# Two unused tiles that move every loaded tile to a multiple of 512 bytes of its partition, in a one-token decoder block

## The chip, the cores and the metric

The kernel runs on one core of a Trainium2 chip. The metric is the device time of one execution in microseconds (us), lower is better. Three runs before the change gave 672.55, 671.69 and 673.35 us, a median of 672.55 us.

## What is computed

One decoding step of a conditioned transformer block for 4 sequences of one token each, with a model width of 512. The condition `c` gives six vectors (shifts, scales and gates). The attention has 32 heads of 128 with a cache of 4096 keys and values for each head and sequence; the caches are 128 MiB each, and every byte of both is read once.

```python
mod = (silu(c) @ w_mod).reshape(4, 6, 1, 512)        # sa, ca, ga, sb, cb, gb
h = layernorm(x) * (1 + ca) + sa
q = (h @ wq) split into 32 heads of 128
p = softmax(q . k_cache / sqrt(128)); o = p . v_cache
x = x + ga * (o @ wo)
h = layernorm(x) * (1 + cb) + sb
z = gelu(h @ w_in); z1, z2 = halves; z2 = layernorm(z2)
x = x + gb * ((z1 * (w_sp * z2 + b_sp)) @ w_out)
```

All arrays are bfloat16.

## The kernel before, in words

The attention is cut into 32 steps (`NT`), one for each pair of four heads and one sequence. A step needs one key tile `kt` and one value tile `vt`, each 128 partitions x 128 rows x 128 numbers of bfloat16: 4096 KB, and 32,768 bytes in one piece for each partition, in HBM as in SBUF. Both names have two buffers (pool `kv`). The order of all work is written out by hand (`manual_schedule`); nothing is rearranged by a scheduler.

In step `i` VectorE multiplies the key tile in place by the queries, in two halves (`mult`, L286, 64 instructions in all). TensorE adds up groups of 8 of the products with an identity matrix as weights, 16 matmuls for each half (`reduce_d`, L292, 1024 in all). VectorE finishes the sum (L301) and takes maxima, ScalarE takes exponentials into `pbd` (L324), and two steps later TensorE multiplies with the value tile (`pv`, L352). As soon as the second half of `reduce_d` of step `i` is issued, the load of key tile `i + 2` is issued into the buffer that step `i` has read (`load_k`, L103), and after `pv(i - 2)` the load of value tile `i` (`load_v`, L103). All these loads go through the queue of SyncE (SP) in the order in which they stand, and an issue that waits for its buffer holds back those behind it.

Ahead of the caches `w_mod` (`wm_sb`, L89) and `wq` (`wq_sb`, L91) are loaded. In step 2 their pool is closed, and `wo_sb` and `wo_last` (L530, L535) are loaded into its place; ahead of the last step the last value tile (in four pieces, `TAIL`), `win_sb` (L552) and `wout_sb` (L554) follow. After the last landing the gated second half of the block is finished (L630 to L695).

SBUF is laid out by pools: first `consts` (constants, `pbd`, queries `qbc` and small vectors), then `kv`, then `work`, and then `pre`, whose place `wts` takes over. Within a pool tiles lie one behind the other, in sizes rounded up to 32 bytes. So the start of every loaded tile follows from the sum of the sizes ahead of it:

| tiles | pool | start in the partition, before | modulo 512 |
|---|---|---|---|
| `kt` (two buffers) | kv | 35,360 and 68,128 | 32 |
| `vt` (two buffers) | kv | 100,896 and 133,664 | 32 |
| `wm_sb`, later `wo_sb` | pre, wts | 169,440 | 480 |
| `wq_sb` | pre | 194,016 | 480 |
| `wo_last`, `win_sb`, `wout_sb` | wts | 198,112, 202,208, 216,544 | 480 |

Of the kernel before, what the change touches and what calls it, by code (L numbers as in the profile page):

```python
# [24 lines left out]
def kernel(  # L25
# [17 lines left out]
    P = 128  # L43
# [21 lines left out]
    consts = ctx.enter_context(tc.tile_pool(name="consts", bufs=1))  # L65
    kvp = ctx.enter_context(tc.tile_pool(name="kv", bufs=2))
    wk = ctx.enter_context(tc.tile_pool(name="work", bufs=2))
# [97 lines left out]
    x1w = consts.tile([P, DJ, R], F32, name="x1w")  # L165
    nc.gpsimd.memset(x1w, 0.0)
    cT = consts.tile([P, DJ, B], BF16, name="cT")
    pbds, opss = [], []
    for k in range(3):
        t = consts.tile([P, NJ, HQ], BF16, name=f"pbd{k}")  # L170
# [555 lines left out]
```

## Time and profile before

| | us |
|---|---|
| median of three runs | 672.55 |
| the profiled execution's own time | 671.79 |
| its span, first to last instruction | 670.0 |
| VectorE busy | 415.3 (62%) |
| TensorE (matmul) busy | 388.6 (58%) |
| ScalarE busy | 85.0 (13%) |
| DMA queue of SyncE, share of 16 DMA engines' span | 98.6% |

The span is what the trace covers; 1.79 us of the profiled execution's time lie around it. Busy times are sums over one engine. The share of the DMA queue is the time that its packets took, divided by 16 times the span, since a core has 16 DMA engines. "GB/s" is what the DMA engines moved in a stretch. In the groups of instructions a row has the line, engine and operation, output and inputs with shapes, the count, the busy time, the mean of one in ns, and the idle time of the engine ahead of them with what ended it.

### The profile page before, as it was taken

The page shows a single profiled execution, that of the slowest core. Times are in us where ns is not written, and L with a number is a line of the kernel's source. Part 1 is how long each engine was busy: PE and PEld are TensorE (multiplying, and loading weights), DVE is VectorE, ACT ScalarE, POOL GpSimd, SP SyncE. Part 2 cuts the span into 40 slices and gives each one's busy share as a digit, 9 for nine tenths or more (in the row PEclk, how much of TensorE's full clock was granted, in tenths as well). Part 3 has the DMA queues.
Part 4 walks back from the last instruction along what each step waited for, and adds up shares of the span by engine and source line. Part 5 has one row for each costly group of instructions (what it writes and reads, how often), then busy time and mean ns, then how long its engine had stood idle before and what let it go on. Part 6 is the DMA issues. An engine that isn't in the chain of part 4 may idle for free.

```text
span 670.0 us, 6859 instructions
## 1 busy us (share of the span) xinstructions
PE 388.6 (58%) x2864; PEld 182.6 (27%) x2864; DVE 415.3 (62%) x594; ACT 85.0 (13%) x278; POOL 3.8 (1%) x17
## 2 busy tenths in 40 slices
PE   1184784455566655646664566566555566556666
PEld 1032332122222322222222233222222233222335
DVE  3185593775555776555577656557765555776833
ACT  1011220111011111101111110111111011111112
POOL 1000000000000000000000000000000000000000
PEclk9998988778988778789877789987777988877975
DMA  9999999999999999999999999999999999999995
GB/s 376 432 432 425 430 418 426 435 434 427 426 435 431 431 428 427 433 430 431 428 433 430 432 426 431 435 426 430 434 430 432 426 431 430 429 432 423 439 413 203
DMA packets 12322, 283.17 MB, mean 423 GB/s; under 512 B 1276, under 2 KB 2692, under 8 KB 3076
## 3 DMA queue, kind: packets, MB, share of 16 engines
q1 hardware_dynamic: 12272, 282.73, 98.6%
q8 instruction: 22, 0.36, 0.2%
q14 instruction: 8, 0.07, 0.0%
q10 hardware_dynamic: 20, 0.01, 0.0%
HBM read 282.73 MB, written 0.00 MB: 422 GB/s over the span
## 4 chain that ended last, share of the span: by engine, by line
DMA 58%; DVE 28%; PE 12%; issue 1%; SPq 0%; DVEq 0%
DMA kt<-in_A_k_cache_dram 53%; DVE kt L286 21%; PE red L292 10%; DMA wout_sb<-in_B_w_out_dram 5%; DVE osb L364 2%; DVE S L301 1%; DVE mrow L310 1%; DVE osb L360 1%; PE ops L352 1%; DVE mt L314 0%; DVE nM L316 0%; PE qps L272 0%; DVE mb L312 0%; DVE nM L317 0%; PE sm L240 0%
## 5 line engine op out<-in xcount | busy, mean ns | idle before, releaser
L292 PE MATMUL red<-kt,ident_bf 128*128 128x512 bf16 x1024 | 292.1, 450 | 251.3 <-DVE kt L286 251.3
L286 DVE TENSOR_TENSOR kt<-kt,qbc 128x8192 bf16<-128x8192 bf16 x64 | 282.8, 4420 | 201.9 <-DMA kt<-in_A_k_cache_dram 201.0
L292 PEld LDWEIGHTS <-ident_bf 128*128 128x128 bf16 x1024 | 116.7, 114 | 419.2 <-issue 275.2
L324 ACT ACTIVATE pbd<-S,nM 32x128 bf16<-32x128 f32 x128 | 73.8, 577 | 508.3 <-DVE rz L344 470.7
L352 PE MATMUL ops<-vt,pbd 128*16 128x512 bf16 x992 | 60.9, 387 | 0.0
L301 DVE TENSOR_REDUCE S<-red 128x64 f32<-128x512 f32 x64 | 43.6, 682 | 5.2 <-PE red L292 5.2
L364 DVE SCALAR_TENSOR_TENSOR osb<-ops,selg,osb 128x128 f32<-128x128 f32 x93 | 32.6, 351 | 3.3
L324 ACT ACTIVATION_READ_ACCUMULATOR pbd<-S,nM 32x1 f32 x128 | 32.0, 250 | 0.0
L352 PEld LDWEIGHTS <-pbd 128*16 128x16 bf16 x992 | 24.1, 90 | 21.6 <-issue 1.7
L372 PEld LDWEIGHTS sm<-sel,osb 128*128 128x128 f32 x62 | 11.9, 198 | 11.1 <-DVE osb L364 4.5
L272 PE MATMUL qps<-wq_sb,hTb 128*32 128x512 bf16 x128 | 9.2, 412 | 9.2 <-DMA wq_sb<-in_A_wq_dram 8.5
L339 PEld LDWEIGHTS sm<-rsb,ones_f 128*128 128x128 f32 x64 | 12.3, 194 | 4.5
L372 PE MATMUL sm<-sel,osb 128*128 128x4 f32 x62 | 9.3, 221 | 5.4 <-DVE osb L364 5.4
L360 DVE TENSOR_SCALAR osb<-ops,selg 128x128 f32<-128x128 f32 x31 | 10.2, 328 | 3.4 <-PE ops L352 3.4
L276 ACT CAST qbc<-qps 128x512 bf16<-128x512 f32 x8 | 4.7, 586 | 46.6 <-PE qps L272 46.6
L310 DVE TENSOR_REDUCE mrow<-S 128x1 f32<-128x128 f32 x32 | 9.1, 286 | 1.1
L339 PE MATMUL sm<-rsb,ones_f 128*128 128x4 f32 x64 | 9.3, 215 | 0.0
L332 DVE TENSOR_SCALAR rsb<-mask,rs 128x4 f32<-128x4 f32 x32 | 7.1, 223 | 2.4 <-ACT pbd L324 2.4
L314 DVE STREAM_TRANSPOSE mt<-mb 128x32 f32<-128x32 f32 x32 | 6.8, 212 | 1.1
L272 PEld LDWEIGHTS <-hTb 128*32 128x32 bf16 x128 | 3.1, 100 | 13.3 <-issue 10.6
L316 DVE TENSOR_REDUCE nM<-mt 128x1 f32<-128x32 f32 x32 | 6.0, 186 | 1.1
L312 DVE COPY mb<-mrow 128x32 f32<-128x32 f32 x32 | 5.8, 181 | 1.1
(129 smaller groups left out, 86.5 us busy)
## 6 DMA issues: line engine op xcount, KB each, us to landing
kt<-in_A_k_cache_dram SPq DMA_DIRECT2D x31, 4096.0 KB, 23.3
vt<-in_A_v_cache_dram SPq DMA_DIRECT2D x31, 4096.0 KB, 30.9
wq_sb<-in_A_wq_dram SPq DMA_DIRECT2D x1, 4096.0 KB
kt<-in_A_k_cache_dram SPq DMA_DIRECT2D x2, 2048.0 KB, 18.3
wm_sb<-in_w_mod_dram SPq DMA_DIRECT2D x1, 3072.0 KB, 10.4
wo_sb<-in_A_wo_dram SPq DMA_DIRECT2D x3, 1024.0 KB, 23.1
kt<-in_A_v_cache_dram SPq DMA_DIRECT2D x1, 2048.0 KB
win_sb<-in_B_w_in_dram SPq DMA_DIRECT2D x1, 1792.0 KB, 33.5
```

What stands on the lines that cost most here:

```text
L272: nc.tensor.matmul(qp[R * q:R * (q + 1)], lhsT=hTb[:, k, b, :], rhs=wq_v[:, k, gs, q, :], start=(k == 0), stop=(k == DJ - 1), tile_positio ...
L286: nc.vector.tensor_tensor(out=kt, in0=kt, in1=bc(qbc[:, g, b, :], KC), op=ALU.mult)
L292: nc.tensor.matmul(red, lhsT=ident_bf, rhs=kt[:, :, m * RD:(m + 1) * RD], start=(m == 0), stop=(m == DH // RD - 1),)
L301: nc.vector.tensor_reduce(out=st[i, "S"][:, kc * KC:(kc + 1) * KC], in_=st.pop((i, "red", kc)), axis=AX.X, op=ALU.add,)
L310: nc.vector.tensor_reduce(out=mrow, in_=S, axis=AX.X, op=ALU.max)
L324: nc.scalar.activation(out=pbd[r, :, q], in_=S[r, :], func=AF.Exp, bias=nM[r, :], scale=att_scale, accum_out=rs[r, :],)
L332: nc.vector.tensor_scalar(out=rsb, in0=mask4, scalar1=st.pop((i, "rs")), scalar2=None, op0=ALU.mult)
L339: nc.tensor.matmul(z, lhsT=ones_f, rhs=st.pop((i, "rsb")), start=True, stop=True)
L352: nc.tensor.matmul(opss[i % 2][g:g + G * HQ], lhsT=pbds[i % 3][:, n, :], rhs=vts[i][:, n, :], start=(m < 4), stop=(m >= NJ // G - 4), tile ...
L360: nc.vector.tensor_scalar(out=osb, in0=ops[:, 0, :], scalar1=selg[:, 0:1], scalar2=None, op0=ALU.mult)
L364: nc.vector.scalar_tensor_tensor(out=osb, in0=ops[:, g, :], scalar=selg[:, g:g + 1], in1=osb, op0=ALU.mult, op1=ALU.add,)
L372: nc.tensor.matmul(op, lhsT=st.pop((i, "osb")), rhs=sel4, start=True, stop=True)
```

## The change

Two tiles are allocated that no instruction writes or reads: one of 480 bytes at the end of what stands ahead of `pbd` in the pool `consts`, and one of 64 bytes in the pool `work`.

```diff
     nc.gpsimd.memset(x1w, 0.0)
     cT = consts.tile([P, DJ, B], BF16, name="cT")
+
+    consts.tile([P, 480], mybir.dt.uint8, name="gap")
+    wk.tile([P, 64], mybir.dt.uint8, name="gap", bufs=1)
     pbds, opss = [], []
     for k in range(3):
```

In the built program everything in `consts` behind `cT`, and the whole pool `kv`, lies 480 bytes further on; everything in `work`, `pre` and `wts` lies 544 bytes further on. `kt` begins at 35,840 and 68,608, `vt` at 101,376 and 134,144, `wm_sb` and `wo_sb` at 169,984, `wq_sb` at 194,560, `wo_last` at 198,656, `win_sb` at 202,752 and `wout_sb` at 217,088, all multiples of 512. The instructions of each engine, their number and their order are the same; line numbers behind the change grow by 3.

## The prediction

> **What bounds the kernel now.** I read the share of the DMA engines first, because the kernel reads 256 MiB of caches for little arithmetic: the rows of 40 slices, the queue, and the list of DMA issues.
>
> ```profile
> DMA  9999999999999999999999999999999999999995
> GB/s 376 432 432 425 430 418 426 435 434 427 426 435 431 431 428 427 433 430 431 428 433 430 432 426 431 435 426 430 434 430 432 426 431 430 429 432 423 439 413 203
> DMA packets 12322, 283.17 MB, mean 423 GB/s; under 512 B 1276, under 2 KB 2692, under 8 KB 3076
> q1 hardware_dynamic: 12272, 282.73, 98.6%
> kt<-in_A_k_cache_dram SPq DMA_DIRECT2D x31, 4096.0 KB, 23.3
> vt<-in_A_v_cache_dram SPq DMA_DIRECT2D x31, 4096.0 KB, 30.9
> ```
>
> The DMA engines are busy in every slice but the last, at much the same rate, and SyncE's queue fills 98.6% of them. A key tile lands 23.3 us after its issue. Its own bytes need 4.194 MB / 430 GB/s = 9.75 us, so some 13.5 us of older transfers stand ahead of it: the queue doesn't run dry. Next, whether that rate depends on what the engines do, by stretches of the span (us, busy time of each engine with its count of instructions, granted TensorE clock, DMA share, GB/s):
>
> ```profile
> core 0: us, PE busy (x) PEld busy (x) DVE busy (x) ACT busy (x) POOL busy (x), PEclk, DMA share, GB/s
> 120.00:620.00 500.00, 293.26 (x1911) 133.55 (x1911) 326.68 (x427) 60.17 (x208) 0.00 (x0) 0.84 1.00 430
> 217.11:256.12 39.01, 24.75 (x200) 12.24 (x200) 25.51 (x34) 4.62 (x16) 0.00 (x0) 0.82 1.01 432
> 404.00:443.00 39.00, 23.19 (x171) 11.05 (x170) 25.58 (x34) 4.65 (x16) 0.00 (x0) 0.87 1.00 428
> 0.00:30.00 30.00, 4.90 (x60) 3.17 (x60) 6.53 (x41) 2.59 (x5) 2.68 (x12) 1.00 0.96 401
> 20.00:30.00 10.00, 1.90 (x16) 0.50 (x15) 0.00 (x0) 0.59 (x1) 0.00 (x0) 1.00 0.99 429
> 629.00:665.00 36.00, 24.25 (x353) 15.48 (x351) 16.27 (x54) 7.95 (x24) 1.08 (x5) 0.68 0.91 378
> ```
>
> For 500 us the rate stays at 430 GB/s with no free DMA time. From 20 to 30 us, with VectorE idle, it is 429. Last, the groups that touch the big tiles, and the chain of waits:
>
> ```profile
> L292 PE MATMUL red<-kt,ident_bf 128*128 128x512 bf16 x1024 | 292.1, 450 | 251.3 <-DVE kt L286 251.3
> L286 DVE TENSOR_TENSOR kt<-kt,qbc 128x8192 bf16<-128x8192 bf16 x64 | 282.8, 4420 | 201.9 <-DMA kt<-in_A_k_cache_dram 201.0
> DVE kt L286 <- DMA kt<-in_A_k_cache_dram: 201.0, 29, 16.9
> 629.29 35.56 DMA wout_sb<-in_B_w_out_dram
> ```
>
> VectorE's multiplication stood idle 201 us for key tiles still in transit, and TensorE in turn waited for VectorE. The last landing, of `wout_sb` at 664.85 us, is followed by 5.15 us of short dependent steps.
>
> The span closes as a sum of transfers. Queue 1's 282.73 MB at 430 GB/s take 657.5 us. The first issues end at 1.64 us. The first 30 us at 401 in place of 430 lose 30 x 29/430 = 2.0 us; the stretch 629 to 665 at 378 loses 36 x 52/430 = 4.4 us. With 5.15 us behind the last landing that makes 670.7 us against 670.0 measured. So one per cent of transfer rate is worth 6.6 us, and an engine's instruction is worth nothing until it outgrows its idle time. The profiled execution took 671.79 us, 1.79 around the span; the median of the runs is 0.76 us above it.
>
> **The change part by part.** *Instructions.* None is added, removed or moved: no wait, no DMA issue, no queue position. This costs zero and needs no cover.
>
> *The engines' operands.* Key, value and query tiles move by the same 480 bytes, from 32 to 0 modulo 64 in the case of `kt`, `vt` and `qbc`, so their distances from each other stay. The trace holds no multiplication at another start: all 64 took 4394 to 4428 ns by tile `kt`'s own list. I can therefore only bound what an aligned start does to it. VectorE is busy about 25.5 us of a 39 us double step with four multiplications; it has 13.5 us to spare, 3.4 us for each, and an instruction of 4.42 us would have to become 77% slower before it set the pace. A faster one gains nothing there, as its tile isn't there earlier. TensorE has 39 - 24.75 = 14.25 us to spare over 64 matmuls of L292, 220 ns for each on top of 450 ns. If that cover were gone, each extra 100 ns of L286 would cost 6.4 us over 64. I put it at zero. A release of the buffer that comes later is covered too, by the 13.5 us of transfers in the queue.
>
> *The tail.* Behind the last landing, 5.15 us consist of small instructions whose tiles shift by 544 bytes, some onto a multiple of 64 and some off it. Bound: 10% of 5.15 us either way, 0.5 us; I take zero, since equal numbers move each way.
>
> *The transfers.* This is the one place where the change can pay. Each partition row of `kt` and `vt` is one piece of 32,768 bytes that started 32 bytes beyond a multiple of 512 and ended 32 bytes beyond one; 31 + 31 full tiles of 4096 KB are 260 of the 282.7 MB. The weights started 32 bytes short of one. No tile in the trace is written at a multiple of 512, so the price of a shifted start isn't seen and has to be bounded. Upper bound of the gain: the fastest slice of the row, 439 GB/s, held throughout: 657.5 x (1 - 430/439) = 13.5 us. But its neighbours are 423 and 413, so that is bytes booked into one slice or the next; the best 39 us stretch that I listed is 432, worth 657.5 x (1 - 430/432) = 3.0 us. Lower bound: a start that all rows share could also do harm; the slowest slice between the first and the last five, 418, held throughout, costs 657.5 x (430/418 - 1) = 18.9 us, and the slowest stretch of 39 us, 428, costs 3.1 us. Between these I take the size of what is misplaced: 32 bytes at the edge of 32,768. If those 32 bytes make one extra piece, as dear as 32 bytes more, the row is 32 / 32,768 = 0.098% longer, 0.64 us over 657.5 us. It is nearest to the stretches, which differ by under half a per cent whatever runs beside them; anything that cost at each 256 or 512 bytes of a row would be many times as much.
>
> The Trainium skill's page "DMA: Bandwidth & Descriptors" says, under "How a descriptor splits into AXI transactions", that a descriptor is cut at 256-byte boundaries, and that bytes ahead of an unaligned start still cost beats of 32 B. By that rule a row of 32,768 bytes at offset 32 has 129 transactions for 128, and I estimate 1025 beats for 1024, 0.64 us in all; no row here shows it. The same page, under "Where 436 GB/s comes from", puts the ceiling of the ports at 435.2 GB/s, and this speaks against the change: the 430 of the long stretch is 1.2% below, so by the page the sum could at best fall by an estimated 7.9 us, and all fixed costs of a transfer would have to vanish for it.
>
> *Sum.* 671.79 - 0.64 = 671.15 us for the profiled execution; for the median, 672.55 - 0.64 = 671.9 us. A measurement of this kernel can tell about 0.3% from no change, 2.0 us: below 670.5 it is faster, above 674.6 slower.
>
> **The rivals.** *The shifted start costs more than its 32 bytes* (say, each row's write is broken at every boundary, or its end needs a second pass). With the rate at 432 the median becomes 672.55 - 3.0 = 669.5 us, at 439 it would be 659. For it: nothing else bounds the kernel, so all of a gain arrives. Against it: a rate that already holds at 428 to 432 in every long stretch looks like a ceiling, not like a stream with breaks in it. It decides from 2.0 us / 512 rows for each DMA engine (64 tiles of 128 rows over 16 engines), about 4 ns of the 1219 ns (9.75 us / 8 rows) that a row takes.
>
> *Writes that start alike meet the engines' accesses* and so slow the transfers. Place: the landing of `kt` and `vt` rows in SBUF while VectorE rewrites one `kt` buffer in place and TensorE reads it and a `vt` buffer, all now at the same place modulo 512. Price: the stretch at 428, 672.55 + 3.1 = 675.6 us; the slice at 418 would make 691. It decides from the same 4 ns a row, in the other direction. Against it: all four buffers lay alike modulo 512 before as well, and the rate is 429 with VectorE idle and 432 with it busy 65% of the stretch.
>
> *The change does nothing*, because an unread tile is dropped or a start has no cost at all: 672.55 us. The addresses of the built program do move, so only the second half of this is open; it lies inside the forecast's band.
>
> **How the numbers follow.** Within 0.3%, by the forecast or by no effect at all: 0.64. The first rival, faster by over 0.3%: 0.24. The second, slower: 0.12. The first outweighs the second because there is at least a plain direction to it. The likeliest case lies between 670.5 and 673.5 us. The range reaches to both rivals' stretch values, 669.5 and 675.6, and somewhat beyond the first, to 668.0, since its price is bounded only by the fastest slice: 668.0 to 675.6 us. About 0.09 is left below and 0.08 above.
>
> **What would show it.** If I am right, the 500 us stretch shows 430 or 431 GB/s again, queue 1 some 98.6%, the idle time of VectorE ahead of L286 stays near 201 us, and L286 and L292 keep their means of 4420 and 450 ns. If the first rival is right, the rate from 120 to 620 us rises to 432 or more, and VectorE's idle time for key tiles falls by as much as the time. If the second is, the rate falls to 428 or below with the DMA share still at 1.00. A new duration of L286 or L292 without a new time would show that the engines feel the start and that the cover holds. Wrong altogether would be a fall of the DMA share: then something other than transfers has become late.

## The result, and the profile after

The changed kernel takes 669.47 us (median of 7 runs, 668.62 to 671.05) against 672.55 us before (again the median, of 7 runs from 671.69 to 673.35): a ratio of 0.9959 with a 95% interval of 0.9947 to 0.9972. It is faster by 3.1 us, 0.41%, and the interval leaves out 1. That is the first rival's time, not the forecast's 671.9. It lies outside the likeliest case of 670.5 to 673.5; the range held it, as it had been drawn out to that rival.

First the 40 slices, the queue, the DMA issues and the groups that touch the key tile, in the page of the changed kernel (its L289 and L295 are L286 and L292 of before):

```profile
span 666.7 us, 6859 instructions
DMA  9999999999999999999999999999999999999995
GB/s 378 438 424 429 432 420 433 437 438 428 432 432 438 428 429 432 439 432 424 440 431 436 427 432 433 437 430 431 434 435 432 427 435 432 435 425 431 439 419 204
q1 hardware_dynamic: 12272, 282.73, 98.6%
kt<-in_A_k_cache_dram SPq DMA_DIRECT2D x31, 4096.0 KB, 23.2
L295 PE MATMUL red<-kt,ident_bf 128*128 128x512 bf16 x1024 | 292.8, 451 | 248.0 <-DVE kt L289 248.0
L289 DVE TENSOR_TENSOR kt<-kt,qbc 128x8192 bf16<-128x8192 bf16 x64 | 282.8, 4420 | 198.1 <-DMA kt<-in_A_k_cache_dram 197.2
```

The same number of instructions and of DMA packets, the same bytes, the same share of 98.6%, and the span is 3.3 us shorter: the same stream runs a little faster. The multiplication keeps its 4420 ns and the matmul has 451 for 450; VectorE waits 3.8 us less for key tiles, which is the gain seen from the consumer's side. By stretches (us, busy time and count of each engine, granted clock, DMA share, GB/s), again the changed kernel:

```profile
0.00:30.00 30.00, 4.87 (x60) 3.16 (x60) 6.53 (x41) 2.59 (x5) 2.69 (x12) 1.00 0.96 402
120.00:620.00 500.00, 296.66 (x1923) 134.70 (x1923) 327.68 (x430) 60.13 (x208) 0.00 (x0) 0.83 1.00 432
```

The 500 us stretch went from 430 to 432 GB/s with the DMA engines busy throughout in both. The first 30 us hardly changed (401 to 402).

The rate is the mean over many rows, and its last digit is too coarse to show where the time went. The trace also holds each row, the piece of a partition that one DMA packet writes, with its duration. Mean durations by size, in ns (rows that took over 5% more than the median, some 30 of 8064 in each kernel, are left out for 8192 bytes and more), and how many of them an engine writes:

```
bytes in the row   rows per engine   before   after   difference
 1024                    88            49.1    46.0      3.1
 4096                    24           162.0   159.0      3.0
 8192                    32           314.4   309.0      5.4
16384                    24           615.5   611.0      4.5
32768                   504          1217.7  1213.1      4.6
```

After the change nearly all rows of a size take the same time: 99% of those of 32,768 bytes have 1213 ns. Before, from 120 to 620 us, not one had 1213: 70% took 1214 to 1216 ns and 28% took 1221 to 1226. The difference doesn't grow in proportion to the length of the row: it is 3.1 ns at 1 KB and 4.6 at 32 KB. Summed by rows it is 504 x 4.6 + 88 x 3.1 + 24 x 3.0 + 32 x 5.4 + 24 x 4.5 ns = 2.9 us for each engine, of the 3.1 us measured. (Two sizes with 8 rows each for an engine, those of `wm_sb` and `win_sb`, are not in the table; with them an engine writes 688 rows of 1 KB and more, for which an expectation below has 704.)

### The profile page after: what moved, and what is told of

The parts are those of the page before. It is cut to its first block, busy times and chain, and to the rows that moved or that the text cites. A ratio compares the mean times of both kernels' runs of the same rounds, so it can differ in the third digit from the quotient of the medians.

```text
span 666.7 us, 6859 instructions
## 1 busy us (share of the span) xinstructions
PE 389.3 (58%) x2864; PEld 182.6 (27%) x2864; DVE 415.4 (62%) x594; ACT 85.0 (13%) x278; POOL 3.8 (1%) x17
## 3 DMA queue, kind: packets, MB, share of 16 engines
q1 hardware_dynamic: 12272, 282.73, 98.6%
## 4 chain that ended last, share of the span: by engine, by line
DMA 54%; DVE 29%; PE 14%; issue 1%; ACT 1%; SPq 0%; DVEq 0%
DMA kt<-in_A_k_cache_dram 54%; DVE kt L289 21%; PE red L295 11%; DVE osb L367 3%; DVE S L304 1%; PE ops L355 1%; DVE mrow L313 1%; DVE osb L363 1%; DVE mt L317 1%; PE qps L382 1%; DVE nM L319 0%; DVE mb L315 0%; PE qps L275 0%; DVE nM L320 0%; PE sm L243 0%
## 5 line engine op out<-in xcount | busy, mean ns | idle before, releaser
L295 PE MATMUL red<-kt,ident_bf 128*128 128x512 bf16 x1024 | 292.8, 451 | 248.0 <-DVE kt L289 248.0
L289 DVE TENSOR_TENSOR kt<-kt,qbc 128x8192 bf16<-128x8192 bf16 x64 | 282.8, 4420 | 198.1 <-DMA kt<-in_A_k_cache_dram 197.2
L295 PEld LDWEIGHTS <-ident_bf 128*128 128x128 bf16 x1024 | 116.8, 114 | 416.6 <-issue 278.9
L375 PEld LDWEIGHTS sm<-sel,osb 128*128 128x128 f32 x62 | 11.9, 198 | 11.2 <-DVE osb L367 4.7
```

Source lines behind the costliest of these rows:

```text
L289: nc.vector.tensor_tensor(out=kt, in0=kt, in1=bc(qbc[:, g, b, :], KC), op=ALU.mult)
L295: nc.tensor.matmul(red, lhsT=ident_bf, rhs=kt[:, :, m * RD:(m + 1) * RD], start=(m == 0), stop=(m == DH // RD - 1),)
L375: nc.tensor.matmul(op, lhsT=st.pop((i, "osb")), rhs=sel4, start=True, stop=True)
```

## The experiments

**Which tiles carry the gain.** Theory A: a start off the boundary costs for every row written, whatever its length. Theory B: the weight tiles at the start and the end carry the gain. In the first kernel the second gap has 32 bytes for 64, so only keys and values are aligned; in the second there is only a gap of 32 bytes in `work`, so only the weights are.

```diff
 kv_only
-    wk.tile([P, 64], mybir.dt.uint8, name="gap", bufs=1)
+    wk.tile([P, 32], mybir.dt.uint8, name="gap", bufs=1)
 weights_only
-    consts.tile([P, 480], mybir.dt.uint8, name="gap")
-    wk.tile([P, 64], mybir.dt.uint8, name="gap", bufs=1)
+    wk.tile([P, 32], mybir.dt.uint8, name="gap", bufs=1)
```

Keys and values alone: 

> Only the key and value tiles begin at a multiple of 512 (480 bytes of gap ahead of them); the weight tiles stay at 480 modulo 512. Theory A (a start off the boundary costs an amount for each row written, whatever its length): 504 of a DMA engine's 704 data rows of 1 KB and more get cheaper, so most of the 3.1 us return: about 669.9 to 670.3 us, with the long stretch at 432 GB/s. Theory B (the weights' tiles carry the gain, in the start and the end of the kernel): 672 to 673 us and 430 GB/s.

Weights alone: 

> Only the weight tiles (w_mod, wq, wo, w_in, w_out) begin at a multiple of 512; the key and value tiles stay at 32 modulo 512. Theory A: a small rest of the gain, 0.3 to 0.9 us, so 671.7 to 672.3 us, with the long stretch at 430 GB/s. Theory B: 669 to 670 us.

Keys and values alone gave 669.51 us, ratio 0.9951 (0.9939 to 0.9964), the whole gain. Weights alone gave 671.12 us, ratio 0.9983 (0.9974 to 0.9992): 1.4 us (0.5 to 1.8), where A had 0.3 to 0.9. Their stretches, first keys and values, then weights:

```profile
120.00:620.00 500.00, 298.93 (x1922) 135.10 (x1922) 327.62 (x430) 60.15 (x208) 0.00 (x0) 0.83 1.00 432
120.00:620.00 500.00, 296.94 (x1911) 134.11 (x1911) 326.68 (x427) 60.23 (x208) 0.00 (x0) 0.81 1.00 430
```

The rate follows the key and value tiles; B is out. The interval of the second kernel reaches into A's band, and its profiled execution gained 0.5 us (671.25 for 671.79). A small part of its gain came from key and value rows: they kept 1213 ns until about 50 us of the span, and again from 87 to 136 us, although they began at 32 modulo 512; only then did they go to a mean of 1217.8 ns for good. By count and difference this is worth an estimated 0.2 us, so it doesn't explain all of the 1.4; the rest of the surplus stays open. What makes that cheap state end is taken up below.

**Whether the engines' own accesses are part of it.** Theory C: writes at such a start lose time only because VectorE and TensorE use SBUF beside them. The kernel has the layout of before and leaves out most of the work on the big tiles, so its output is not the block's.

```diff
-        nc.vector.tensor_tensor(out=kt, in0=kt, in1=bc(qbc[:, g, b, :], KC), op=ALU.mult)
 ...
-        for m in range(DH // RD):
-            nc.tensor.matmul(
-                red, lhsT=ident_bf, rhs=kt[:, :, m * RD:(m + 1) * RD],
-                start=(m == 0), stop=(m == DH // RD - 1),
-            )
+        nc.tensor.matmul(
+            red, lhsT=ident_bf, rhs=bc(ident_bf[:, 0:RD], KC), start=True, stop=True
+        )
 ...
-        for m in range(NJ // G):
+        for m in range(4):
 ...
-                start=(m < 4), stop=(m >= NJ // G - 4), tile_position=(0, g),
+                start=True, stop=True, tile_position=(0, g),
```

> The layout of before, with the engines taken off the big tiles: the multiplication by the queries is left out, one matmul on the identity stands for the sixteen on the key tile, and 4 of the 32 matmuls on the value tile are left. If the start costs a fixed amount by itself (theory A in its plain form), the rows of 32,768 bytes take a mean of 1218 ns as before, and the long stretch has 430 GB/s. If writes at such a start lose time only where engines read and write SBUF beside them (theory C), they take 1213 ns and the stretch has 432 GB/s.

The engines' busy times on its page, and the long stretch:

```profile
PE 108.5 (16%) x1036; PEld 66.2 (10%) x1036; DVE 141.1 (21%) x530; ACT 84.5 (13%) x278; POOL 3.8 (1%) x17
120.00:620.00 500.00, 67.25 (x465) 39.64 (x465) 105.42 (x377) 59.84 (x208) 0.00 (x0) 0.50 1.00 431
```

TensorE's busy share fell from 58% to 16% and VectorE's from 62% to 21%, and rows of 32,768 bytes still took 1217.9 ns from 120 to 620 us, to the tenth as before, with the same groups at 1216 and 1224. C is out for the engines' work on the key and value tiles: without any on the key tiles, and with an eighth of the matmuls on the value tiles, the loss is the same. ScalarE's share didn't change (13%), so this kernel says nothing of its accesses. The stretch has 431 GB/s for 430, and the one run took 670.76 us. Part of both lies in long rows: 15 rows of 32,768 bytes took over 5% more than the median, for 29 before, worth some 0.5 us for each engine. The shorter program also fetches less code (8 packets on the instruction queue q8 for 22); that this makes fewer long rows was not shown.

**Which boundary counts.** First all buffers on different multiples of 64, by a gap ahead of each buffer:

```diff
+            if i == 1:
+                kvp.tile([P, 64], mybir.dt.uint8, name="gap_kt1", bufs=1)
-            kts[i] = kvp.tile([P, NJ, DH], BF16, name="kt", bufs=2)
+            kts[i] = kvp.tile([P, NJ, DH], BF16, name=f"kt{i % 2}", bufs=1)
 ...
+        if i < 2:
+            kvp.tile([P, (64, 128)[i]], mybir.dt.uint8, name=f"gap_vt{i}", bufs=1)
-        vts[i] = kvp.tile([P, NJ, DH], BF16, name="kt" if i == L else "vt", bufs=2)
+        vts[i] = kvp.tile([P, NJ, DH], BF16, name="kt0" if i == L else f"vt{i % 2}", bufs=1)
 ...
-    wk.tile([P, 64], mybir.dt.uint8, name="gap", bufs=1)
```

> The two key buffers begin at 0 and 64 modulo 512, the two value buffers at 128 and 256, the weights at 192: all multiples of 64, one of them of 512. If 64 bytes are enough, as much as the change: 669.5 us, and every 32,768-byte row of the long stretch takes the same time. If 256 or 512 are needed, half or three quarters of the rows stay dear: 671 to 672 us, and the row times fall into as many groups as there are starts.

669.31 us, ratio 0.9953 (0.9941 to 0.9966): the whole gain, though three of four buffers lay off 512. Taken alone this would have made 64 bytes the rule, and that would have been wrong. The rows were not all alike: in loads of the buffer at 64 they took 1214.6 ns in the mean, at 256 some 1213.8, at 128 1213.1 and at 0 1213.0. The loads come in the order 0, 128, 64, 256, so the buffer at 256 comes after the dearest one and that at 128 after an aligned one: a mixture can't price a start by itself. So every start was then given to all four buffers at once, by the sizes of the two gaps (480 and 64 in the change): 32 and 0 for a start at 64; 96 and 448 for 128; 224 and 320 for 256. For a start 16 bytes beyond a multiple of 64 each buffer got 64 bytes more and was used from its byte 16 on (`vt` likewise, without the gap in `work`):

```diff
-            kts[i] = kvp.tile([P, NJ, DH], BF16, name="kt", bufs=2)
+            t = kvp.tile([P, NJ * DH + 32], BF16, name="kt", bufs=2)
+            kts[i] = t[:, 8:8 + NJ * DH].rearrange("p (n d) -> p n d", d=DH)
```

At 64: 

> All four cache buffers begin at 64 modulo 512 (modulo 128 too), the weights at multiples of 512. If a multiple of 64 is enough: 669.5 us and rows of 1213 ns. If the boundary is 128 or more: the rows keep a mean near 1218 ns, and the time is that of the kernel with only the weights aligned, 671 to 672 us. In the run with four starts the buffer at 64 had rows of 1214.6 ns in the mean and that at 128 had 1213.0, which speaks for a part of the cost.

At 128: 

> All four cache buffers begin at 128 modulo 512, the weights at multiples of 512. If the boundary is 64 or 128: 669.5 us, rows of 1213 ns. If it is 256 or 512: 671 to 672 us, rows near 1218 ns.

At 256: 

> All four cache buffers begin at 256 modulo 512, the weights at multiples of 512. If the boundary is 256 or less: 669.5 us, rows of 1213 ns. If only 512 will do: 671 to 672 us, rows near 1218 ns.

At 16 beyond a multiple of 64: 

> All four cache buffers begin 16 bytes beyond a multiple of 64 (and not at a multiple of 32, as all starts so far), the weights at 192 modulo 512. If the cost is one more piece of a row at its end, whatever the start: as before, 672 to 673 us, rows of 1218 ns. If a start off 32 bytes costs for each piece of a row, the rows grow by several per cent (1240 ns or more) and the time passes 680 us.

Last, starts at multiples of 32,768, with the three `pbd` tiles moved from `consts` into a pool behind `kv`:

```diff
+    late = ctx.enter_context(tc.tile_pool(name="late", bufs=1))
 ...
-        t = consts.tile([P, NJ, HQ], BF16, name=f"pbd{k}")
+        t = late.tile([P, NJ, HQ], BF16, name=f"pbd{k}")
```

> The three tiles pbd of 1024 bytes are moved behind the cache buffers, which so begin at 32,768, 65,536, 98,304 and 131,072; the weights lie as in the change. If only the boundary of 256 bytes counts: the same as the change, 669.5 us, rows of 1213 ns. If coarser boundaries count too (a row that lies within one block of 32,768 bytes and crosses fewer of them), rows below 1213 ns and a time below 668.5 us; this would be the best version.

The mean row of 32,768 bytes from 120 to 620 us, and the time; each ratio is to runs of the kernel before that were taken together with it (medians 672.71 us, and 672.49 for the last row):

```
start of the four buffers            row, ns   time, us   ratio to before (95% interval)
32 modulo 512 (before)                1217.9    672.55
16 beyond a multiple of 64            1217.5    671.99    0.9992 (0.9983 to 1.0001)
64 modulo 512                         1216.6    671.33    0.9978 (0.9968 to 0.9988)
128 modulo 512                        1216.6    670.44    0.9966 (0.9953 to 0.9978)
256 modulo 512                        1213.0    668.74    0.9945 (0.9933 to 0.9957)
0 modulo 512 (the change)             1213.0    669.47    0.9959 (0.9947 to 0.9972)
0 modulo 32,768                       1213.0    669.12    0.9952 (0.9939 to 0.9964)
```

The stretches of the starts at 128 and at 256:

```profile
120.00:620.00 500.00, 295.82 (x1912) 133.63 (x1912) 327.22 (x430) 60.08 (x208) 0.00 (x0) 0.83 1.00 431
120.00:620.00 500.00, 298.54 (x1923) 135.00 (x1923) 327.98 (x430) 60.19 (x208) 0.00 (x0) 0.82 1.00 432
```

Rows at 256 are as good as at 512 and at 32,768, and at 128 and 64 they are still slowed: the boundary is 256 bytes. It is the rows that show it. The time at 128, 670.44 us, lies between the two values expected for it; the weights are aligned there too, the cache rows had 1213 ns again for some 50 us (below), and all its rows sum to 1.3 us less than before for each engine, where the two profiled executions differ by 1.4. At 64 the rows are as long as at 128; the 0.9 us between their times can't be put down to the start, as the profiled execution at 64 had a gap in its stream (352 GB/s from 76 to 80 us, 410 at 128). The three aligned kernels can't be told apart by their intervals. A start off 32 bytes is no worse than one at 32, so nothing is paid for each piece of a row. The Trainium skill's page "DMA: Bandwidth & Descriptors", under "How a descriptor splits into AXI transactions", cuts descriptors at just 256 bytes. It words this for reads, and these rows are writes into SBUF; the boundary agrees with them. The cost that follows from its beats does not: its one extra beat in 1024 is an estimated 0.1% of a row, 1.2 ns, and the rows of before lost 4.9 ns, or nothing at all in the first 23 us of the span.

**Whether each row pays.** Key and value tiles are loaded by four transfers each, with the layout of before and with that of the change:

```diff
-            load(kts[i], kv_view(A_k_cache, i), (KC, NJ - KC) if i == L else (NJ,))
+            load(kts[i], kv_view(A_k_cache, i), (KC, NJ - KC) if i == L else 4 * (NJ // 4,))
 ...
-        load(vts[i], kv_view(A_v_cache, i), TAIL if i == L else (NJ,))
+        load(vts[i], kv_view(A_v_cache, i), TAIL if i == L else 4 * (NJ // 4,))
```

Layout of before: 

> The layout of before, with each full key and value tile loaded by four transfers of 1024 KB, so that a partition's 32,768 bytes arrive as four rows of 8192 bytes, each beginning at 32 modulo 512. More rows cost time in both layouts (a row of 8192 bytes took 309 ns in the changed kernel, four of them 23 ns more than one of 32,768: about 11 us over 496 tile rows of an engine, and some 2 us for the added transfers). If the misplaced start costs for each row, it is paid four times: 9 to 12 us above the aligned twin, near 694 us. If it costs for bytes or for time, 3 us above it, near 686 us.

Layout of the change: 

> The layout of the change, with each full key and value tile loaded by four transfers of 1024 KB, rows of 8192 bytes at multiples of 512. Both theories: about 669.5 + 13 = 682 to 684 us, with rows of 309 ns; what tells them apart is the distance to the kernel with the same split and the old layout.

687.93 us (ratio 1.0233, 1.0219 to 1.0247) and 676.69 us (1.0066, 1.0054 to 1.0079). Both fell below the expectation by 5 to 7 us, since it added the rows' durations, and the records of successive rows overlap: early in the trace rows of 1213 ns begin 1209.5 ns apart. But their distance is 11.2 us, in the 9 to 12 that a price for each row gives, and 3.6 times the 3.1 us of whole rows. The rows of 8192 bytes took 314.5 and 309.0 ns from 120 to 620 us. The stretches, layout of before first:

```profile
120.00:620.00 500.00, 292.06 (x1893) 132.27 (x1893) 314.32 (x415) 57.89 (x200) 0.00 (x0) 0.81 1.01 420
120.00:620.00 500.00, 295.97 (x1911) 133.89 (x1910) 322.44 (x426) 60.13 (x208) 0.00 (x0) 0.82 1.01 427
```

With short rows the same 32 bytes cost 1.6% of the rate for 0.5%.

**What stays open.** In all kernels with whole tiles, whatever the start, at least 97% of the rows of 32,768 bytes in the first 23 us of the span take 1213 ns (128 of some 176 are those of `wq_sb`), and the rows of 8192 bytes of both split kernels take a mean of 309.0 there. Misplaced starts begin to cost between 25 and 70 us of the span, gradually. The cost also went away again in four kernels. Mean rows of 32,768 bytes in ns, by stretches of the span; between the second and the third column `wo_sb` and `wo_last` land (97 to 110 us):

```
start of the buffers, of the weights   GB/s, 76-80 us   88-97   110-136   150-620
32, off (before)                                  418   1217.6    1217.9    1217.9
16 beyond 64, off                                 352   1213.3    1217.7    1217.5
32, aligned (weights alone)                       385   1213.4    1213.4    1217.9
64, aligned                                       352   1213.4    1213.2    1216.8
128, aligned                                      410   1216.4    1213.4    1216.8
```

Where the stream had a gap (352 and 385 GB/s), the rows behind it took 1213 ns; where the weights were aligned, they took 1213 ns behind the weights, with or without a gap before; after 136 to 150 us the cost was back. So a misplaced start makes a row open to a loss that builds up over tens of us of such rows, and that a gap or some us of aligned rows seem to clear. The buffers with four starts fit this. These are single traces, read afterwards, and no run was made that holds that state on purpose: what the state is stays open.

## Why the prediction was right and wrong

The frame held. The transfers carry the time: an edit that changes no instruction moved the time by 3.1 us, nearly all of it by the transfer rate, and the DMA share, L286, L292 and the queue's depth stayed as forecast. The operands' new starts cost the engines nothing (4420 ns before and after), so the cover of 3.4 us for each multiplication was not needed. The tail is nearly the same too, with one change at its head. In the timelines of before and after, the first matmul group on `wout_sb` (the brackets give the idle time and what ended it):

```profile
664.90 0.91 PE L658 MATMUL qps<-zz,wout_sb 128*128 128x8 bf16 x28 [0.38 <-DMA wout_sb<-in_B_w_out_dram]
661.47 0.89 PE L661 MATMUL qps<-zz,wout_sb 128*128 128x8 bf16 x28 [0.21 <-DVE zz L654]
```

Before, it waited for the last landing; now the landing is earlier and it waits for VectorE. The chain that ended last has this as its last transfer in the changed kernel:

```profile
601.91 18.52 DMA kt<-in_A_k_cache_dram
```

It leaves the transfers at 620.43 us, with the last landing of a key tile (before, VectorE waited for that one until 623.34 us), and runs through the engines for the 46 us behind it. The prediction's sum had the bytes of that stretch on the path (its 4.4 us for 629 to 665 us). A saving on what lands after that key tile should now bring nothing more, which was not run.

The step that failed is the size of one term in *The transfers*: "If those 32 bytes make one extra piece, as dear as 32 bytes more, the row is 32 / 32,768 = 0.098% longer". That makes 1.2 ns a row and 0.64 us; the runs showed 4.6 to 4.9 ns and 3.1 us. What speaks for a cost at the edge of a row: the price is much the same for rows of 1 KB and of 32 KB (3.1 and 4.6 ns), it is paid nearly four times when a row is cut into four, and it goes away at a boundary of 256 bytes. But its price isn't that of its bytes, and an extra piece alone can't be the cause, since misplaced rows early in the span took 1213 ns; what it is stays open. It lay above the 4 ns from which, by the prediction's own working, the first rival decides.

That rival's value with the rate at 432, 669.5 us, is what was measured, but this was luck. The 432 came from one stretch of 39 us (217 to 256 us), and the 428 beside it from another (404 to 443 us); in both, rows of 32,768 bytes took 1217.9 ns. The two rates differ by the bytes that were booked in or out, and 432 happens to be what the stream reaches when the loss is gone.

The reason given against that rival was weak: that a rate of 428 to 432 in every long stretch "looks like a ceiling". An even rate shows that the loss is even, not that there is none. The single rows of the trace of before had the answer: rows of one size took 1213 ns at first and 1214 to 1226 later, which no ceiling explains. The stretch of 20 to 30 us at 429 GB/s, which was to show that the engines don't matter, was too short to be read so closely. Bytes are booked by packet: from 12 to 30 us the rate reads 435 before and 437 after, though the rows there take the same time in both.

```profile
12.00:30.00 18.00, 2.30 (x28) 0.92 (x26) 1.27 (x6) 0.59 (x1) 0.00 (x0) 1.00 1.01 435
12.00:30.00 18.00, 2.07 (x22) 0.69 (x19) 1.27 (x6) 0.59 (x1) 0.00 (x0) 1.00 1.01 437
```

What it was to show is right all the same, by the kernel with idle engines. The second rival, a loss by writes that start alike, found nothing: starts alike modulo 512, and even modulo 32,768, gave rows of 1213.0 ns.

## What to carry to other kernels

Where a kernel streams from HBM at its full rate, let the destination of every large transfer begin at a multiple of 256 bytes of its partition; an unread tile of the right size in front of the pool does it, and it costs no instruction. Only the side in SBUF was moved here; starts in HBM were not varied. The gain is a few ns for each contiguous row and engine, so count the rows: 0.4% with rows of 32 KB, 1.6% with rows of 8 KB, and where transfers have time to spare there should be nothing to gain, which was not run. And when a term is the price of one row, look at the durations of single rows in the trace, early and late, before calling an even rate a ceiling.

## What the runs showed of the hardware that was not expected

A row that is written at a multiple of 256 takes the same time nearly always (1213 ns in 99% of the changed kernel's 8064 rows), while before, at 32 modulo 512, it took 1214 to 1226 from 120 to 620 us, with two clear groups, 1216 and 1224. The loss doesn't come at once: rows at 32, 64, 128 or 16 had 1213 ns for the first 23 us of the span (97% of them or more), and it went away for some 50 us behind a gap in the stream or behind aligned rows. And starts mix: a buffer at 128 modulo 512 cost next to nothing (1213.1 ns) where its loads took turns with buffers at 0, 64 and 256, but 1216.6 ns where all four lay at 128, and the time of that mixture, 669.31 us, can't be told from that of four aligned buffers.
